# Gate tables with one operand in PSUM, whole-piece weight differences, and two batches' score transposes side by side

## The chip, the cores and the metric

The kernel runs on one core of a Trainium2 chip. The metric is device time in microseconds (us), taken as the median of several runs. With it comes one profiled execution, whose trace says when every instruction started and how long it took. The engines are TensorE (PE, with its weight loads as PEld), VectorE (DVE), ScalarE (ACT), GpSimd (POOL), and SyncE (SP), which starts most transfers. SBUF is the on-chip memory that all of them share, and PSUM the accumulator memory that TensorE writes.

## The reference

```python
def _attn_ref(x, w_r, w_i, b_r, b_i):        # x: 8 x 2496 x 256
    X = np.fft.rfft(x, axis=1)
    Yr = Xr @ w_r - Xi @ w_i + b_r
    Yi = Xr @ w_i + Xi @ w_r + b_i
    Yr = np.sign(Yr) * np.maximum(np.abs(Yr) - 0.01, 0.0)      # Yi alike
    return np.fft.irfft(Yr + 1j * Yi, n=2496, axis=1)

def _moe_ref(x, w_gate, w1, w2, capacity):   # x: 19968 x 256, 8 experts, capacity 80
    logits = x @ w_gate
    expert_idx = np.argmax(logits, axis=1)
    probs = np.exp(logits - logits.max(-1, keepdims=True))
    probs /= probs.sum(-1, keepdims=True) + 1e-09
    gate_w = probs[np.arange(N), expert_idx]
    out = np.zeros((N, D))
    for e in range(E):
        tok_idx = np.where(expert_idx == e)[0]
        # more than capacity: keep the 80 with the largest gate_w
        h = np.maximum(x[tok_idx] @ w1[e], 0.0)          # w1[e]: 256 x 1024
        out[tok_idx] = gate_w[tok_idx, None] * (h @ w2[e])
    return out
```

A Fourier transform along the sequence, a complex linear layer with a soft threshold, the way back, and then a mixture of eight experts in which each serves at most 80 of the 19968 tokens. All other rows of the output are zero.

## The kernel before, in words

**Main loop.** The sequence of 2496 is split as 39 x 64. The loop has 16 steps, two for each of the eight batches (`b` 0 to 7), and pipelines stages: a 39-point transform in f32, a 64-point transform, the complex weights with the soft threshold (L384 on TensorE; L392, L398, L401 on the others), and the way back, whose last part (`stageHB`, L534, L568, L572, with results in tiles `hs`) goes to the DRAM arrays `hd`. The step between, `stageD`, is L477, L480, L481 and L509 on TensorE with evictions L487 and L492 into `YO`.

**Gate tables.** The logits are linear in x, so the kernel carries eight gate columns through the inverse transform beside the data. For each batch `stageE1a` sums the gate columns to `G` and splits it into an f16 pair, `stageE1b` transforms them and sends them through DRAM (`gd`) to `gr`, and `stageE2` turns them into a table. A TensorE matmul leaves the logits L (78 partitions x 256, that is 32 tokens of 8 experts) in a PSUM tile. Then come the maximum `m` (L709), `d = L - m` (L710), `exp` on ScalarE (L711), its sum `q` (L712) and reciprocal (L713, L714), and the first place that holds the maximum, found with a table of ranks (L716, L717, L718). The last operation (L719) writes the gate of each token at its expert's place into the table, tile `gr`, or `Gs` for batch 6. `stageE3` transposes the table on TensorE (L725) and copies it from PSUM into `sall`, where all batches' tables lie side by side (L728 on VectorE for batches 6 and 7). Batch 7 goes by a path of its own, `stageG0`, `stageG1`, `stageE1c` and `back`, without the way through DRAM.

**Selection.** After the last table, VectorE selects tokens in `sall`: `level1` (L855 maxima, L856 their places, L864 products with a table `mod` into `V`, which TensorE L865 moves to the expert rows), index arithmetic on 128x16 tiles (L821 to L844), and rounds of maximum, replace and find (L882, L887, L888). `merge` and `choose` end it with L928, and TensorE turns its result into token positions (L933). Then GpSimd gathers rows by indirect transfers (L1020), TensorE runs the experts (L1105 and on), and the rows are scattered to the output (L1162).

**Weights.** Each expert's w1 and w2 come as f32 in four units of 128x1024. ScalarE makes the f16 part `wh` (L780; L777 and L774 for late ones), and the difference `wl = w - wh` in bf16 is GpSimd's (L788), for four units VectorE's (L783). Both parts lie in a tile `pair`.

**What sets the order.** The program is traced by a scheduler that keeps a modelled timeline. `tc.high_priority()` lets the instructions traced in it go ahead, and `tc.issue_after` holds instructions back until a named one has been placed. Each engine then executes its list strictly in order. PSUM tiles come from `psum()`, a ring of four buffers of 128x1024 f32; a buffer is free for its next user once the last instruction that reads or writes it is done.

Of the kernel before, what the change touches and what calls it, by code (L numbers as in the profile page):

```python
# [132 lines left out]
def fourier_mix_then_moe(ctx, tc, x, w_r, w_i, b_r, b_i, wg, w1, w2, t1, t2, vq, v3, v0, v1f, vt, sg, cst, cb, out):  # L133
    nc = tc.nc
# [4 lines left out]
    ek = ctx.enter_context(tc.tile_pool(name="ek", bufs=1))  # L139
# [18 lines left out]
    def psum():  # L158
        return ps[0].tile([128, 1024], F32, name="ps", bufs=ps[1])
# [17 lines left out]
    rank = const.tile([128, 8], F32, name="rank")  # L177
# [9 lines left out]
    unit = const.tile([128, 1], F32, name="unit")  # L187
# [170 lines left out]
    twos = []  # L358
# [223 lines left out]


    def stageE1a(b, Gs):
        G = ek.tile([128, 20, 8], F32, name="G", bufs=1)
        nc.vector.tensor_reduce(out=G, in_=Gs.rearrange("p c q (h e) -> p c e (q h)", e=8), op=ALU.add, axis=AX.X)
        gp = ek.tile([128, 2, 20, 8], F16, name="gp", bufs=2)
        nc.scalar.activation(gp[:, 0], G, AF.Copy)
        nc.vector.tensor_tensor(gp[:, 1], G, gp[:, 0], op=ALU.subtract)
        return gp  # L590

    v1h = const.tile([39, 78], F32, name="v1h")
    u7s = []
    uh7 = const.tile([128, 2, 5, 24], F16, name="uh7")

    def stageG0(b, YT):

        pt = psum()
        for j in range(11):
            c = j if j < 2 else 2 + (j + 4) % 9  # L600
            for eh in range(2):
                yt = lambda h: YT[:, eh, h, j].rearrange("p c k -> p (c k)")
                nc.tensor.matmul(pt[:, 16 * c:16 * c + 16], yt(0), wgi[:, eh, 128:144], start=(eh == 0), stop=False)
                nc.tensor.matmul(pt[:, 16 * c:16 * c + 8], yt(1), wgi[:, eh, 128:136], start=False, stop=(eh == 1))
        G = ek.tile([128, 20, 8], F32, name="gex")[:, :11]
        gp = ek.tile([128, 2, 20, 8], F16, name="gp", bufs=2)[:, :, :11]
        nc.vector.tensor_reduce(out=G, in_=pt[:, 0:176].rearrange("p (c h e) -> p c e h", h=2, e=8), op=ALU.add, axis=AX.X)
        nc.scalar.activation(gp[:, 0], G, AF.Copy)
        nc.vector.tensor_tensor(gp[:, 1], G, gp[:, 0], op=ALU.subtract)
        return gp  # L610

    def stageG1(b, R, eh):

        pt = psum()
        pv = pt[:, 0:120].rearrange("p (t k e) -> p t k e", t=5, k=3)
        for k in range(3):
            for x in range(3):
                nc.tensor.matmul(pv[:, :, k], R[:, 3 * x + k].rearrange("p c k -> p (c k)"), wgm[:, eh, x], start=(x == 0), stop=(x == 2))
        pv = pt[:, 0:120].rearrange("p (t f) -> p t f", t=5)
        if eh == 0:  # L620
            u7s.append(ek.tile([128, 20, 8], F32, name="G", bufs=1).rearrange("p a b -> p (a b)")[:, :120].rearrange("p (t f) -> p t f", t=5))
            nc.vector.tensor_copy(u7s[0], pv)
        else:
            u7 = u7s[0]
            nc.vector.tensor_tensor(u7, pv, u7, op=ALU.add)
            nc.scalar.activation(uh7[:, 0], u7, AF.Copy)
            ones.append(nc.vector.tensor_tensor(uh7[:, 1], u7, uh7[:, 0], op=ALU.subtract))

# [6 lines left out]
    def stageE1b(b, gp):  # L635
        pt = psum()

        for t, (tab, k) in enumerate(((vqs, 2), (vis, 8), (vqs, 14))):
            for v, h in ((0, 0), (0, 1), (1, 0)):
                nc.tensor.matmul(pt[:, 48 * t:48 * t + 48], tab[:, v], gp[:, h, k:k + 6, :], start=(v + h == 0), stop=(v == 1))  # L640
        special(pt[:64, 512:536], gp)
        gh = ek.tile([128, 21, 8], F32, name="gh", bufs=1)
        gu = ek.tile([128, 2, 48], F32, name="gdif")
        sc = 2.0 / S / XS
        g = float(np.sqrt(0.75))
        at = lambda a: gh[:, 6 * a:6 * a + 6].rearrange("p k e -> p (k e)")
        nc.scalar.activation(at(0), pt[:, 0:48], AF.Copy, scale=sc)
        nc.scalar.activation(gu, pt[:, 48:144].rearrange("p (t f) -> p t f", t=2), AF.Copy, scale=sc)
        nc.scalar.activation(gh[:64, 18:21], pt[:64, 512:536].rearrange("p (a e) -> p a e", a=3), AF.Copy, scale=sc)
        nc.vector.scalar_tensor_tensor(gu[:, 1], gu[:, 1], -1.5, at(0), op0=ALU.mult, op1=ALU.add)  # L650
        for a, f in ((1, g), (2, -g)):
            nc.vector.scalar_tensor_tensor(at(a), gu[:, 0], f, gu[:, 1], op0=ALU.mult, op1=ALU.add)
        nc.sync.dma_start(gd[b][0:21].rearrange("q n e -> n q e"), gh[0:64])
        nc.sync.dma_start(gd[b][21:39].rearrange("q n e -> n q e"), gh[64:128, 0:18])
        gr = ek.tile([78, 32, 8], F32, name="gr", bufs=1)
        for h in range(2):
            hops.append(nc.sync.dma_start(gr[39 * h:39 * h + 39], gd[b][:, 32 * h:32 * h + 32, :]))
        return gr
# [36 lines left out]
    def stageE2(b, gr, last=False):  # L695
        pt = psum()
        if last:
            for h in range(2):
                nc.tensor.matmul(pt[:78, :256], v1h if h else v1fs[:39], gr[:, :, 32 * h:32 * h + 32], start=(h == 0), stop=(h == 1))
        else:  # L700
            nc.tensor.matmul(pt[:78, :256], v1fs, gr.rearrange("p n e -> p (n e)"), start=True, stop=True)
        L = pt[:78, :256].rearrange("p (e n) -> p n e", e=8) if last else pt[:78, :256].rearrange("p (n e) -> p n e", e=8)
        bc = lambda t: t.unsqueeze(2).to_broadcast([78, 32, 8])
        m = ek.tile([78, 32], F32, name="gm")
        d = ek.tile([78, 32, 8], F32, name="gdif")
        ex = ek.tile([78, 32, 8], F32, name="gex")
        q = ek.tile([78, 32], F32, name="gq")
        sc = wkb.tile([128, 20, 2, 16], F32, name="Gs", bufs=2)[:78].rearrange("p a b c -> p (a b c)")[:, :256].rearrange("p (e n) -> p e n", e=8) if b == B - 2 else ek.tile([78, 8, 32], F32, name="gr", bufs=1)
        nc.vector.tensor_reduce(out=m, in_=L, op=ALU.max, axis=AX.X)  # L709
        nc.vector.tensor_tensor(d, L, bc(m), op=ALU.subtract)  # L710
        exps.append(nc.scalar.activation(ex, d, AF.Exp))  # L711
        nc.vector.tensor_reduce(out=q, in_=ex, op=ALU.add, axis=AX.X)  # L712
        nc.vector.scalar_tensor_tensor(q, q, 1e-9, unit[:78, 0:1].to_broadcast([78, 32]), op0=ALU.add, op1=ALU.mult)  # L713
        nc.vector.reciprocal(q, q)  # L714
        rk = rank[:78].unsqueeze(1).to_broadcast([78, 32, 8])
        nc.vector.scalar_tensor_tensor(d, d, 0.0, rk, op0=ALU.is_ge, op1=ALU.mult)  # L716
        nc.vector.tensor_reduce(out=m, in_=d, op=ALU.max, axis=AX.X)  # L717
        nc.vector.tensor_tensor(d, d, bc(m), op=ALU.is_equal)  # L718
        twos.append(nc.vector.tensor_tensor(sc.rearrange("p e n -> p n e"), d, bc(q), op=ALU.mult))  # L719
        return sc  # L720

    def stageE3(b, sc):
        pt = psum()
        for h in range(2):
            nc.tensor.transpose(pt[:, 128 * h:128 * h + 78], sc[:, 4 * h:4 * h + 4].rearrange("p e n -> p (e n)"), ident[:78, :78])  # L725
        o, i = sall[:, :, b], pt[:, :256].rearrange("p (h f) -> p h f", h=2)[:, :, :78]
        if b >= B - 2:
            nc.vector.tensor_copy(o, i)  # L728
        else:
            nc.scalar.activation(o, i, AF.Copy)  # L730
# [11 lines left out]
    def prepW(e, pool, name):  # L742
# [20 lines left out]
        def step(k, i):  # L763
# [4 lines left out]
            wh, wl = pairs[e][:, 0], pairs[e].bitcast(BF16)[:, 1]  # L768
            load(k, i)
            wt = got[k, i]  # L770
            c = 1024 * i
# [9 lines left out]
            if (e, k, i) in WV:  # L781
                with behind(("A", 'xv', (3, 4)[k])) if e == 7 and after else tc.issue_after(sels[-1].ins):
                    nc.vector.tensor_tensor(wl[:, k, c:c + 1024], wt, wh[:, k, c:c + 1024], op=ALU.subtract)  # L783
            else:

                m = 256 if e >= 2 else 1024
                for j in range(0, 1024, m):
                    nc.gpsimd.tensor_tensor(wl[:, k, c + j:c + j + m], wt[:, j:j + m], wh[:, k, c + j:c + j + m], op=ALU.subtract)  # L788
        return [(e, lambda k=k, i=i: step(k, i), lambda k=k, i=i: load(k, i)) for k in range(2) for i in range(2)]

    def weight(e, k):
# [699 lines left out]
    HBq.extend((pb, YO, pch, x) for x in (0, -1, 1, 2))  # L1491
    with tc.high_priority():
        sc = stageE2(b, gr, True)
    stageE3(p[0], sc6)
    doHB()
    YO1 = YO
    YO = wkb.tile([128, 2, 11, 256], F16, name="YO", bufs=2)
# [1 line left out]
        stageD(1, RR, YO, Gs, cls, False)  # L1499
    doHB(HBE)  # L1500
    with tc.high_priority():
        stageE3(b, sc)
    doHB(2)
    with tc.high_priority():
# [88 lines left out]
```

## Time and profile before

| | us |
|---|---|
| runs (median) | 637.53, 642.4, 640.14 (640.14) |
| the profiled execution | 635.39 |
| span of its instructions | 633.6 |
| outside the span | 1.8 |
| mean granted clock of TensorE | 0.931 of full |
| TensorE busy | 546.1 (86%) |
| VectorE busy | 406.7 (64%) |
| GpSimd busy | 315.2 (50%) |
| ScalarE busy | 302.7 (48%) |

Times in rows are from the start of the span. The main loop fills it to about 515; from there to 560 the tables of batches 6 and 7 and the selection run, and from 560 to the end gather, experts and scatter.

### The profile page before, as it was taken

Reading aid. Unit: us, or ns where it says so; the run is one execution under the profiler, and the core shown is the slowest. Engines: PE = TensorE matmul, PEld = TensorE weight load, DVE = VectorE, ACT = ScalarE, POOL = GpSimd, SP = SyncE. Lnnn points to the kernel's source line nnn. Section 1 sums busy time; section 2 is a strip of 40 time slices with the busy share of each in tenths; the row PEclk is TensorE's granted clock in tenths of the full one; section 3 lists DMA queues with packets and bytes.
Section 4 is the critical chain, followed back from the end, with each engine's and each line's share of the span. In section 5 each row is a group of like instructions: output and inputs, shape, how many; then the busy total and the mean of one; then the engine's idle time right before and its main releaser. Section 6 shows DMA issues by size and latency. Waiting matters only on the chain. (4 is left out here: it accounts for less than half of the span.)

```text
span 633.6 us, 12704 instructions
## 1 busy us (share of the span) xinstructions
PE 546.1 (86%) x4925; PEld 383.8 (61%) x4926; DVE 406.7 (64%) x748; ACT 302.7 (48%) x442; POOL 315.2 (50%) x310
## 2 busy tenths in 40 slices
PE   7366959999999999999999989987899984968791
PEld 2144527676766776686767657765677772526681
DVE  3432525466667667578656996875998847866860
ACT  2322525554545464554446544545566753601560
POOL 2000444444445453544445344575974697647681
PEclk8786978999999999999999999998999975969997
DMA  7796779689679968987997789699754584628830
GB/s 170 268 210 159 205 201 285 196 227 253 200 219 273 267 182 192 304 254 187 249 243 228 199 213 268 169 257 263 238 151 116 150 273 155 204 54 293 297 107 31
DMA packets 95912, 133.12 MB, mean 210 GB/s; under 512 B 26494, under 2 KB 77717, under 8 KB 93973
## 3 DMA queue, kind: packets, MB, share of 16 engines
q1 hardware_dynamic: 88341, 114.59, 67.2%
q10 hardware_dynamic: 5376, 8.39, 4.6%
q0 software_dynamic: 2128, 9.25, 4.3%
q8 instruction: 41, 0.67, 0.4%
q14 instruction: 26, 0.21, 0.1%
HBM read 69.57 MB, written 62.63 MB: 209 GB/s over the span
## 5 line engine op out<-in xcount | busy, mean ns | idle before, releaser
L384 PE MATMUL ps<-XT,WM 128*128 128x288 f16 (+1 forms) x1536 | 217.0, 298 | 8.0 <-DVE R L398 4.7
L384 PEld LDWEIGHTS <-WM 128*128 128x128 f16 x1536 | 149.2, 98 | 66.6 <-issue 12.8
L401 POOL TENSOR_TENSOR R<-R,sgs 128x576 f32<-128x576 f32 x28 | 35.8, 1280 | 183.5 <-DVE R L398 183.4
L398 DVE SCALAR_TENSOR_TENSOR R<-ps,thr,tp 128x674 f32<-128x674 f32 (+1 forms) x56 | 48.4, 864 | 96.1 <-ACT tp L392 94.0
L424 POOL TENSOR_TENSOR YT<-R,YT 128x1408 f16<-128x1408 f32 (+1 forms) x28 | 73.5, 2624 | 36.3 <-ACT YT L423 36.3
L392 ACT ACTIVATE tp<-ps,thr 128x674 f32<-128x674 f32 (+1 forms) x64 | 49.7, 777 | 87.5 <-PE ps L384 87.2
L282 PE MATMUL ps<-xt,t1f 117*117 117x512 f32 (+1 forms) x170 | 86.2, 634 | 3.9 <-DMA xt<-in_x 3.9
L328 PE MATMUL ps<-t2s,z 128*128 128x128 f16 (+1 forms) x320 | 60.3, 225 | 28.8 <-DMA z<-zd 21.1
L297 DVE TENSOR_TENSOR zs<-ps,zs 117x1024 f16<-117x1024 f32 (+1 forms) x45 | 51.0, 1135 | 27.2 <-ACT zs L296 26.1
L334 DVE TENSOR_TENSOR XT<-ps,XT 128x640 f16<-128x640 f32 (+2 forms) x64 | 51.9, 814 | 15.1 <-ACT XT L333 15.1
L296 ACT ACTIVATE zs<-ps 117x1024 f16<-117x1024 f32 (+1 forms) x45 | 43.0, 957 | 38.8 <-PE ps L282 34.7
L333 ACT ACTIVATE XT<-ps 128x640 f16<-128x640 f32 (+2 forms) x64 | 44.9, 702 | 33.9 <-PE ps L330 22.7
L329 PE MATMUL ps<-t2s,z 128*128 128x128 f16 (+1 forms) x320 | 60.2, 225 | 0.0
L330 PE MATMUL ps<-t2s,z 128*128 128x128 f16 (+1 forms) x320 | 60.1, 225 | 0.0
L328 PEld LDWEIGHTS <-z 128*128 128x128 f16 (+1 forms) x320 | 32.1, 100 | 37.5 <-DMA z<-zd 21.2
L423 ACT ACTIVATE YT<-R 128x1408 f16<-128x1408 f32 (+1 forms) x28 | 35.5, 1268 | 36.2 <-POOL R L420 35.9
L534 PE MATMUL ps<-YO,vqs 128*128 128x512 f16 (+1 forms) x252 | 49.5, 338 | 3.3 <-DVE R L398 3.3
L492 DVE TENSOR_TENSOR YO<-ps,YO 128x768 f16<-128x768 f32 (+1 forms) x50 | 45.3, 906 | 5.2 <-ACT YO L491 5.2
L282 PEld LDWEIGHTS ps<-xt,t1f 117*117 117x117 f32 (+1 forms) x170 | 29.2, 188 | 31.4 <-issue 30.3
L481 PE MATMUL ps<-wgi,YT 128*128 128x136 f16 (+1 forms) x302 | 42.8, 225 | 1.0 <-POOL YT L424 1.0
L534 PEld LDWEIGHTS <-vqs 128*128 128x128 f16 x252 | 24.9, 101 | 30.6 <-issue 14.4
L480 PE MATMUL ps<-wgi,YT 128*128 128x144 f16 (+1 forms) x302 | 43.2, 229 | 0.0
(274 smaller groups left out, 939.9 us busy)
## 6 DMA issues: line engine op xcount, KB each, us to landing
out<-zero SPq DMA_DIRECT2D x48, 384.0 KB
hd<-hs SPq DMA_DIRECT2D x94, 192.0 KB
zd<-zs SPq DMA_DIRECT2D x114, 156.0 KB
xt<-in_x SPq DMA_DIRECT2D x48, 312.0 KB
z<-zd SPq DMA_DIRECT2D x16, 576.0 KB
wt<-in_moe_w ACTq DMA_DIRECT2D x10, 512.0 KB
z<-zd SPq DMA_DIRECT2D x7, 704.0 KB
z<-zd SPq DMA_DIRECT2D x7, 640.0 KB
```

The source lines that it names most:

```text
L282: nc.tensor.matmul(pt[:K, 512 * j:512 * j + 512], t1f[:K, :K], xv[:, 2 * j:2 * j + 2], start=True, stop=True)
L297: nc.vector.tensor_tensor(zs[:K, :ng, 1, :], pv[:K, :ng], zs[:K, :ng, 0, :], op=ALU.subtract)
L328: nc.tensor.matmul(o, zz(0), t2s[:K, cl, 0, :], start=True, stop=False)
L329: nc.tensor.matmul(o, zz(0), t2s[:K, cl, 1, :], start=False, stop=False)
L330: nc.tensor.matmul(o, zz(1), t2s[:K, cl, 0, :], start=False, stop=True)
L334: nc.vector.tensor_tensor(ov(1), pv, ov(0), op=ALU.subtract)
L384: nc.tensor.matmul(pt[:, 512 * k:512 * k + n], WM[:, dh, m, wh, 128 * eh:128 * eh + 128], XT[:, dh, xh, c, c0 + n * k:c0 + n * k + n], sta ...
L392: nc.scalar.activation(fv(t), pv, AF.Relu, bias=thr[:, eh, ri, 0:1])
L398: nc.vector.scalar_tensor_tensor(fv(Rf), pv, thr[:, eh, ri, 1:2], fv(t), op0=ALU.add, op1=ALU.min)
L424: nc.gpsimd.tensor_tensor(yv(1), rv, yv(0), op=ALU.subtract)
L492: dvs.append(nc.vector.tensor_tensor(yol, yy, yoh, op=ALU.subtract))
L534: nc.tensor.matmul(o, tab[:, v], yo(h), start=(i == 0), stop=(i == 2))
```

## The change

There are five edits. Lines in the changed kernel are up to three higher or lower: `stageE2` there is L708 to L722, and `stageE3` is L728 and L731.

1. `stageE1a`, `stageG0`, `stageG1`: the sum `G` (or `u7`) goes to PSUM instead of SBUF. `stageE1a` takes a `psum()` buffer for it; the other two use free columns of a buffer that they hold.
2. `stageE1b`: ScalarE's scaled copy of 128x96 (L648) is gone, and VectorE's three operations read the PSUM tile.
3. `stageE2`: the chain for the first place starts from L again and works on PSUM tiles `best` and `place` beside L; the sum goes to PSUM as well. One operation is split in two, so that there are ten VectorE operations instead of nine. The three for the first place stand before the sum of the exponentials. The PSUM buffer is held to the last operation.
4. GpSimd's difference of a unit is one operation of 128x1024 for all experts; for experts 2 and up it was four of 128x256.
5. Batch 6's `stageE3` is written just ahead of batch 7's.

```diff
@@ stageE1a
-        G = ek.tile([128, 20, 8], F32, name="G", bufs=1)
+        G = psum()[:, :160].rearrange("p (c e) -> p c e", e=8)
@@ stageG0
-        G = ek.tile([128, 20, 8], F32, name="gex")[:, :11]
+        G = pt[:, 512:600].rearrange("p (c e) -> p c e", e=8)
@@ stageG1
-            u7 = u7s[0]
-            nc.vector.tensor_tensor(u7, pv, u7, op=ALU.add)
+            u7 = pt[:, 512:632].rearrange("p (t f) -> p t f", t=5)
+            nc.vector.tensor_tensor(u7, pv, u7s[0], op=ALU.add)
@@ stageE1b
-        nc.scalar.activation(gu, pt[:, 48:144].rearrange("p (t f) -> p t f", t=2), AF.Copy, scale=sc)
-        nc.vector.scalar_tensor_tensor(gu[:, 1], gu[:, 1], -1.5, at(0), op0=ALU.mult, op1=ALU.add)
+        nc.vector.scalar_tensor_tensor(gu, pt[:, 96:144], -1.5 * sc, at(0), op0=ALU.mult, op1=ALU.add)
         for a, f in ((1, g), (2, -g)):
-            nc.vector.scalar_tensor_tensor(at(a), gu[:, 0], f, gu[:, 1], op0=ALU.mult, op1=ALU.add)
+            nc.vector.scalar_tensor_tensor(at(a), pt[:, 48:96], f * sc, gu, op0=ALU.mult, op1=ALU.add)
@@ stageE2
-        nc.vector.tensor_reduce(out=q, in_=ex, op=ALU.add, axis=AX.X)
-        nc.vector.scalar_tensor_tensor(q, q, 1e-9, unit[:78, 0:1].to_broadcast([78, 32]), op0=ALU.add, op1=ALU.mult)
+
+        best, place, = (pt[:78, 256 * k:256 * k + 256].rearrange("p (n e) -> p n e", e=8) for k in (1, 2))
+        qs = pt[:78, 768:800]
+        rk = rank[:78].unsqueeze(1).to_broadcast([78, 32, 8])
+        nc.vector.tensor_tensor(best, L, bc(m), op=ALU.is_ge)
+        nc.vector.tensor_tensor(place, best, rk, op=ALU.mult)
+        nc.vector.tensor_reduce(out=m, in_=place, op=ALU.max, axis=AX.X)
+        nc.vector.tensor_tensor(best, place, bc(m), op=ALU.is_equal)
+        nc.vector.tensor_reduce(out=qs, in_=ex, op=ALU.add, axis=AX.X)
+        nc.vector.tensor_scalar(q, qs, 1e-9, None, op0=ALU.add)
         nc.vector.reciprocal(q, q)
-        rk = rank[:78].unsqueeze(1).to_broadcast([78, 32, 8])
-        nc.vector.scalar_tensor_tensor(d, d, 0.0, rk, op0=ALU.is_ge, op1=ALU.mult)
-        nc.vector.tensor_reduce(out=m, in_=d, op=ALU.max, axis=AX.X)
-        nc.vector.tensor_tensor(d, d, bc(m), op=ALU.is_equal)
-        twos.append(nc.vector.tensor_tensor(sc.rearrange("p e n -> p n e"), d, bc(q), op=ALU.mult))
+        twos.append(nc.vector.tensor_tensor(sc.rearrange("p e n -> p n e"), best, bc(q), op=ALU.mult))
@@ step
-                m = 256 if e >= 2 else 1024
-                for j in range(0, 1024, m):
-                    nc.gpsimd.tensor_tensor(wl[:, k, c + j:c + j + m], wt[:, j:j + m], wh[:, k, c + j:c + j + m], op=ALU.subtract)
+                nc.gpsimd.tensor_tensor(wl[:, k, c:c + 1024], wt, wh[:, k, c:c + 1024], op=ALU.subtract)
@@ the end of the main program
-    stageE3(p[0], sc6)
     doHB()
...
     with tc.high_priority():
+        stageE3(p[0], sc6)
         stageE3(b, sc)
```

**What moves.** On TensorE at the end of the main loop, before: `back` (L689), the logits of batches 6 and 7 (L699, tables `v1fs` and `v1h`), then at once the transposes of batch 6's table `Gs`.

```order
7502 L689 MATMUL ps<-ident,Gs 39x64 x8
7503 L699 MATMUL ps<-hs_6211,v1fs 78x256
7504 L699 MATMUL ps<-hs_6211,v1h 78x256
7505 L725 MATMUL ps<-ident,Gs 128x78 x2
7506 L568 MATMUL ps<-YO,v3s 128x512
7507 L568 MATMUL ps<-YO,v3s 128x256
7508 L477 MATMUL ps<-ident,R 128x128 x18
7509 L509 LDWEIGHTS v0s
...
7529 L509 LDWEIGHTS v0s
7530 L509 MATMUL ps<-YO,v0s 64x256
7531 L725 MATMUL ps<-ident,gr 128x78 x2
```

The same place now, on TensorE:

```order
7502 L688 MATMUL ps<-ident,Gs 39x64 x8
7503 L698 MATMUL ps<-hs_6186,v1fs 78x256
7504 L698 MATMUL ps<-hs_6186,v1h 78x256
7505 L568 MATMUL ps<-YO,v3s 128x512
7506 L568 MATMUL ps<-YO,v3s 128x256
7507 L477 MATMUL ps<-ident,R 128x128 x18
7508 L509 LDWEIGHTS v0s
...
7531 L509 MATMUL ps<-YO,v0s 64x256
7532 L728 MATMUL ps<-ident,Gs 128x78 x2
7533 L728 MATMUL ps<-ident,gr 128x78 x2
```

The transposes of batch 6 moved behind L568, L477 and all twelve L509, to stand directly ahead of batch 7's. Nothing stands between the logits and L568 any more.

On VectorE, the chains of batches 6 and 7 before, from the sum of batch 6's exponentials on:

```order
499 L712 TENSOR_REDUCE gq<-gex 78x32
500 L716 SCALAR_TENSOR_TENSOR gdif<-gdif,rank 78x256
501 L713 SCALAR_TENSOR_TENSOR gq<-gq,unit 78x32
502 L717 TENSOR_REDUCE gm<-gdif 78x32
503 L714 RECIPROCAL gq<-gq 78x32
504 L718 TENSOR_TENSOR gdif<-gdif,gm 78x256
505 L709 TENSOR_REDUCE gm<-ps 78x32
506 L719 TENSOR_TENSOR Gs<-gdif,gq 78x32x8
507 L710 TENSOR_TENSOR gdif<-ps,gm 78x256
508 L728 COPY sall<-ps 128x2x78
```

The two chains now, on VectorE (`ps<-` is an operation that writes PSUM; L690 is the copy of `back`):

```order
504 L715 TENSOR_TENSOR ps<-ps,gm 78x256
505 L690 COPY hs_6186<-ps 39x512
506 L716 TENSOR_TENSOR ps<-ps,rank 78x256
507 L717 TENSOR_REDUCE gm<-ps 78x32
508 L718 TENSOR_TENSOR ps<-ps,gm 78x256
509 L708 TENSOR_REDUCE gm<-ps 78x32
510 L709 TENSOR_TENSOR gdif<-ps,gm 78x256
511 L715 TENSOR_TENSOR ps<-ps,gm 78x256
512 L719 TENSOR_REDUCE ps<-gex 78x32
513 L716 TENSOR_TENSOR ps<-ps,rank 78x256
514 L720 TENSOR_SCALAR gq<-ps 78x32
```

The first-place operations of batch 6 stand ahead of its sum (row 512, L719), and the maximum and difference of batch 7 stand ahead of that sum too. Both copies into `sall` (L731) follow at rows 523 and 524, with the selection behind them.

On GpSimd, the last units ahead of the first gather, before and then now:

```order
187 L788 TENSOR_TENSOR pair_5779<-pair_6097,pair_5779 128x256 x8
188 L788 TENSOR_TENSOR pair_6550<-pair_6097,pair_6550 128x256 x12
189 L788 TENSOR_TENSOR pair_6575<-wt,pair_6575 128x256 x4
190 L788 TENSOR_TENSOR pair_6550<-pair_6097,pair_6550 128x256 x4
191 L1020 DMA tok<-cid,posA 128x4 x2
```

```order
186 L788 TENSOR_TENSOR pair_5779<-pair_6080,pair_5779 128x1024 x2
187 L788 TENSOR_TENSOR pair_6501<-wt,pair_6501 128x1024 x2
188 L788 TENSOR_TENSOR pair_6514<-pair_6080,pair_6514 128x1024 x4
189 L788 TENSOR_TENSOR pair_6527<-wt,pair_6527 128x1024
190 L1020 DMA tok<-cid,posA 128x4 x2
```

The same seventeen units stand between the main loop and the first gather, 68 pieces before and 17 now.

## Rows read from the trace of the kernel before

**Rows 1.** Windows, main loop: length; PE, PEld, DVE, ACT, POOL busy; clock; DMA share; GB/s

```profile
177.40:234.80 57.40, 57.23 (x500) 40.38 (x498) 38.64 (x57) 30.96 (x45) 27.77 (x25) 1.00 0.87 237
```

**Rows 2.** Timeline of PE, 520 to 545: start, duration, what ended its idle time

```profile
522.64 1.05 PE L699 MATMUL ps<-hs,v1h 39*78 39x256 f32 x2
532.85 0.52 PE L725 MATMUL ps<-ident,Gs 78*128 78x78 f32 x2 [9.16 <-DVE Gs L719]
533.17 2.85 PE L568 MATMUL ps<-YO,v3s 128*128 128x512 f32 x4
...
540.80 0.35 PE L725 MATMUL ps<-ident,gr 78*128 78x78 f32 x2
```

**Rows 3.** Windows, from batch 7's logits to the last transposes

```profile
522.50:539.00 16.50, 7.34 (x24) 5.08 (x23) 12.27 (x17) 6.34 (x10) 12.22 (x20) 0.50 0.51 157
```

**Rows 4.** Timeline of DVE, 523 to 537, the gate chains

```profile
524.42 6.38 DVE L716 SCALAR_TENSOR_TENSOR gdif<-gdif,rank 78x256 f32<-78x256 f32 x1
...
531.88 0.42 DVE L709 TENSOR_REDUCE gm<-ps 78x32 f32<-78x256 f32 x1
...
534.13 0.41 DVE L716 SCALAR_TENSOR_TENSOR gdif<-gdif,rank 78x256 f32<-78x256 f32 x1
...
535.77 0.97 DVE L719 TENSOR_TENSOR gr<-gdif,gq 78x256 f32<-78x256 f32 x1
```

**Rows 5.** Timeline of POOL, 503 to 549: weight differences

```profile
504.21 3.65 POOL L788 TENSOR_TENSOR pair<-pair,pair 128x256 bf16<-128x256 f32 x4 [4.07 <-ACT pair L780]
...
525.46 5.04 POOL L788 TENSOR_TENSOR pair<-pair,pair 128x256 bf16<-128x256 f32 x8
534.79 8.03 POOL L788 TENSOR_TENSOR pair<-pair,pair 128x256 bf16<-128x256 f32 x12 [4.28 <-ACT pair L777]
...
545.65 2.60 POOL L788 TENSOR_TENSOR pair<-pair,pair 128x256 bf16<-128x256 f32 x4
```

**Rows 6.** Timeline of DVE, 541 to 560, the selection

```profile
541.19 0.32 DVE L728 COPY sall<-ps 128x156 f32<-128x156 f32 x1 [4.45 <-PE ps L725]
...
542.79 0.93 DVE L864 TENSOR_TENSOR V<-mod,cv 128x256 f32<-128x256 f32 x1
...
545.76 0.59 DVE L827 SCALAR_TENSOR_TENSOR tk<-tk,tk 128x16 f32<-128x16 f32 x1
...
548.45 0.14 DVE L821 SCALAR_TENSOR_TENSOR tk<-tk,unit 128x16 f32<-128x16 f32 x1
...
559.10 0.81 DVE L928 TENSOR_TENSOR Gs<-pfb,eye 8x640 f16<-8x640 f32 x1
```

**Rows 7.** Waits of PE, 500 to 560: us in total, times, longest

```profile
PE ps L933 <- DVE Gs L928: 4.3, 1, 4.3
```

**Rows 8.** Groups by form, POOL: count, busy us, mean ns, idle before

```profile
L788 POOL TENSOR_TENSOR pair<-pair,pair 128x256 bf16<-128x256 f32 x48 | 34.1, 743 | 10.5 <-ACT pair L780 6.2 <-ACT pair L777 4.3
...
L788 POOL TENSOR_TENSOR pair<-wt,pair 128x1024 bf16<-128x1024 f32 x8 | 17.2, 2144 | 5.0 <-ACT pair L780 5.0
```

**Rows 9.** Groups by form, DVE, the same operation from PSUM and from SBUF

```profile
L710 DVE TENSOR_TENSOR gdif<-ps,gm 78x256 f32<-78x256 f32 x8 | 3.3, 414 | 0.2
...
L718 DVE TENSOR_TENSOR gdif<-gdif,gm 78x256 f32<-78x256 f32 x8 | 3.0, 381 | 0.0
```

**Rows 10.** Line L492: operation, count, duration ns min/median/max, first and last start, forms

```profile
L492 DVE TENSOR_TENSOR YO<-ps,YO x50: 680/948/959, 104.5 to 508.6; 128x768 f16<-128x768 f32 x42, 128x512 f16<-128x512 f32 x8
```

**Rows 11.** Line L719: the same columns

```profile
L719 DVE TENSOR_TENSOR gr<-gdif,gq x7: 600/2783/2805, 179.8 to 535.8; 78x256 f32<-78x256 f32 x7
```

**Rows 12.** Waits of PE, 230 to 420 (main loop)

```profile
PE ps L725 <- DVE hs L541: 1.4, 1, 1.4
PE ps L384 <- DVE hs L541: 1.4, 3, 0.5
```

**Rows 13.** Timeline of DVE, 502 to 508, ahead of batch 7's gates

```profile
502.44 0.76 DVE L409 TENSOR_TENSOR R<-R,sgs 128x576 f32<-128x576 f32 x1
...
506.29 1.04 DVE L409 TENSOR_TENSOR R<-R,sgs 128x576 f32<-128x576 f32 x1
```

More of the change, by code (lines that the diff above doesn't have):

```diff
@@ L642, in stageE1b @@
         gh = ek.tile([128, 21, 8], F32, name="gh", bufs=1)
-        gu = ek.tile([128, 2, 48], F32, name="gdif")
+        gu = ek.tile([128, 48], F32, name="gdif")
         sc = 2.0 / S / XS
```

## The prediction

> **What bounds the kernel now.** I read the busy shares by stretch first. In the main loop TensorE is the bound, 57.23 of 57.40 us in a typical stretch [rows 1], so VectorE work saved there is worth only what TensorE waits for. Behind the loop it is different, so I went to TensorE's timeline. The logits of batch 7 end at 522.64 + 1.05 = 523.69, and then TensorE sits idle for 9.16 us until it can transpose batch 6's table [rows 2]. All work behind that matmul waits with it, and runs afterwards at half clock: L568 at 533.17 to batch 7's transposes at 540.80, 7.63 us [rows 2]. The granted clock of that stretch is 0.50, the lower of its two levels [rows 3]. VectorE's timeline names the cause. L716 of batch 6 takes 6.38 us; the same operation for batch 7, with GpSimd between two runs, takes 0.41 [rows 4]. L716 reads two SBUF operands, and it begins and ends inside GpSimd's pieces: the last run of them ends at 525.46 + 5.04 = 530.50 [rows 5], and L716 ends at 524.42 + 6.38 = 530.80. Batch 7's chain, whose logits had been there since 523.69, starts at 531.88 behind it [rows 4].
>
> From there one chain of VectorE work sets the time: the last copy into `sall` at 541.19, the selection, its last operation L928 at 559.10 [rows 6], for which TensorE waits 4.3 us [rows 7], then the gather. I take the 73.6 us from there to the end of the span (633.6) as unchanged. So the question is by how much L928 comes earlier.
>
> **Step 1: the tables of batches 6 and 7 (edits 3 and 5).** Do the new chains escape the wait? In the trace of before, the 50 evictions L492 read one PSUM and one SBUF operand in a loop where GpSimd is busy half the time, and the longest takes 959 ns against a median of 948 [rows 10]. L719, with two SBUF operands, ranges from 600 to 2805 [rows 11]. Every operation of the new chain has at most one SBUF operand, so I take it as free of such waits. Its cost: batch 7's chain ran from 531.88 to the start of its last operation at 535.77 [rows 4], 3.9 us, with an operation and a copy of batch 6 among it (some 0.9) and 0.5 us for the last to add; I take 3.5 us for nine operations and 4 for ten. PSUM operands add 414 - 381 = 33 ns each [rows 9], 0.7 us over 20 operations. The two chains together take some 8.5 us and begin at about 522.5, so both tables are ready near 531. TensorE meanwhile does its 7.63 us from 523.69 on, still at half clock, and comes to the transposes at 531.3. Two transposes and two copies (0.52 and 0.35, 0.32 each) end near 533. Before, the second copy ended at 541.51: 8.5 us earlier.
>
> [...]
>
> What could take part of it back is the work ahead of batch 7's gates. L409 at 506.29 took 1.04 instead of the usual 0.76 us, because it met a GpSimd piece [rows 13]; with whole pieces it can meet 2.14 us instead of 0.74 [rows 8]. Bounds for what that and its neighbours delay: nothing and 3.4 us (two whole pieces less what they already wait); I take 1, the value nearest to the row. That leaves about 7.5 us at the second copy.
>
> **Step 2: GpSimd's whole pieces (edit 4).** A unit costs 4 x 0.743 = 2.97 us in pieces on average and 2.14 whole [rows 8]. In the tail, the ten units from 504.21 to 530.50 took 26.3 us and the five from 534.79 to 548.25 took 13.5 [rows 5]. Whole, the ten end at about 525.6. The five wait for ScalarE's copies, which before stood behind the exponential of batch 7, held back by L716; they will come a few us earlier, and with 5 x 2.14 = 10.7 us GpSimd ends at about 542.5 instead of 548.25. ScalarE's pace can put that anywhere between 540 and 545.
>
> **Step 3: the selection meets the pieces.** This is where most of step 1 goes. The selection's operations still have two SBUF operands. Before, while GpSimd worked, L864 took 0.93 and L827 0.59 us; when it had ended, the like of them took 0.14 (L821 at 548.45) [rows 6]. Each waited about one small piece. After, the first L864 is due near 534, and GpSimd works until 542.5. If each waits for one whole piece, L864, L864, L823 and L821 end at about 536, 538.3, 540.4 and 542.6, and L827 starts there instead of at 545.76: 3.1 us earlier. Behind it the rest runs free, which saves the waits of 0.4 us that two or three of them still had before. I take 3.5 us for L928. Lower bound: the first L864 is kept until GpSimd ends, as L716 was; then it ends at 542.9 instead of 543.72, and the operations behind save their waits of 0.3 to 0.5 us each, in all 2.5. Upper bound: it gets in wherever it asks, then all 7.5 us and some of today's waits arrive, about 9.
>
> [...] L716 was kept out for some 6 us, over nine pieces of 5.04 / 8 = 0.63 [rows 4, 5]. [...]
>
> **Step 4: the main loop (edits 1 to 3).** L719 loses about 2.2 us of waiting per batch on VectorE [rows 11], but with TensorE full that shows only where TensorE waits for VectorE behind it: 1.4 us once at L725, and 1.4 in three short waits [rows 12]. Bounds 0 and 2.8; I take 1.5. The ScalarE copy that `stageE1b` loses stands beside TensorE work: nothing. The PSUM buffers of `stageE1a`, `stageE1b` and `stageE2` are held longer, by one chain of about 4 us of VectorE work per batch. The ring has three other buffers meanwhile; I take nothing, and 2 us as a bound on the bad side.
>
> **Step 5: after 560.** Expert 7's differences on GpSimd get 3 x 0.8 = 2.4 us shorter. Nothing shown waits for them: nothing.
>
> **Sum.** 3.5 + 1.5 = 5.0 us. The profiled execution, 635.39 with its 1.8 us outside the span, would come to 630.4. It is 4.75 below the median of 640.14; against the median the forecast is 635.1. The runs spread by 4.9 us, so I treat 1% (6.4 us) as about what a measurement of this kernel can tell from no change.
>
> **Rivals.** *A, the selection gets in freely.* GpSimd's pieces become gaps when ScalarE cannot keep up, and an operation that waits gets in at once. For it: before, all operations of the selection got in at the next boundary [rows 6]. Against it: five whole pieces fall right into it. Then 9 + 1.5 us: 629.6.
>
> *B, all given back.* GpSimd's end stays at 548 because ScalarE's copies come no earlier, the selection waits for it, and main loop and weights are paced by transfers. For it: the idle time ahead of GpSimd's runs is all ScalarE's [rows 5, 8]. Against it: what held ScalarE back hung on L716. It gives 639 to 640.
>
> *C, slower: whole pieces starve VectorE ahead of batch 7's gates.* At 504 to 508 L407 and L409 have two SBUF operands, and ten units follow there without a gap [rows 5]. If L409 is kept out of the run, as L716 was, the gates of batch 7 and all of their work wait. It decides from a delay of 5 us on, more than two whole pieces; kept to the end of the ten units, 525.6 instead of 507.3, it costs 18.3 less the 5.0 gained: 653. Three or four pieces (6.4 to 8.6) give 641.5 to 643.7. Against it: the same operations got in at the first boundary before [rows 13].
>
> *D, the chains are not freed.* Operations with one PSUM operand would wait for GpSimd too, and for whole pieces. Each of the twenty could lose 2 us, TensorE would wait at its transposes until 540 or later, and the time would be 641 or so. L492 [rows 10] speaks against it.
>
> **How the numbers follow.** Forecast 0.42 (632 to 638), A 0.22 (626 to 632), B 0.20 (638 to 641.5), C 0.11, D 0.05. The range 627.5 to 642 leaves out C's greater part, some of D and the end of A, under 0.2. Faster by over 1% means below 633.7: nearly all of A and a third of the forecast, 0.35. Slower by over 1% means above 646.5: 0.08, the long end of C. The rest, 0.57, is within 1%.
>
> **What would show it.** L715 to L722 at 0.2 to 0.5 us each, whatever GpSimd does. TensorE without the 9 us gap, the transposes of 6 and 7 together at 531 to 533. GpSimd's pieces at 2.1 us, the last ending at 540 to 545. L864, L823, L821 at up to 2.2 us each, and L928 at 555 to 557 on the profiled execution's scale. The prediction is wrong if L928 moves by over 7 us or not at all, if L409 takes over 3 us, or if the stretch after L933 changes in length, since I left it as it is.

## The result and the profile after

| | before | after |
|---|---|---|
| runs, first comparison | 639.52 (637.53 to 642.4, 4 runs) | 632.54 (630.13 to 640.27, 4 runs) |
| ratio, 95% interval | | 0.9862 [0.9823, 0.9902] |
| again, with more runs (e1) | 643.9 (640.39 to 649.57, 35 runs) | 638.34 (635.42 to 644.05, 12 runs) |
| ratio, 95% interval | | 0.9907 [0.9876, 0.9938] |
| profiled execution, span | 635.39, 633.6 | 632.38, 630.5 |

Ratios leave out runs that lie over 1.5% above the fastest of their kernel: 640.27 here, three of twelve in e3 and two of twelve in e4. By the medians the change gains 7.0 us, by the larger comparison 643.9 x 0.0093 = 6.0, between 4 and 8. The forecast was 5.0. The profiled execution of the kernel before, 635.39, is faster than any of its 67 runs on record (the lowest is 636.0), while that of the changed kernel lies at its median; so the two profiles differ by less than the runs do.

TensorE after, in the place of [rows 2] (timeline: start, duration, what ended the idle time):

```profile
523.90 0.59 PE L698 MATMUL ps<-hs,v1h 39*78 39x256 f32 x2
524.42 1.56 PE L568 MATMUL ps<-YO,v3s 128*128 128x512 f32 x4
...
528.48 1.53 PE L477 MATMUL ps<-ident,R 128*128 128x128 f32 x12 [1.85 <-ACT hs L578]
529.85 1.59 PE L509 MATMUL ps<-YO,v0s 128*128 128x256 f16 x12
531.37 0.35 PE L728 MATMUL ps<-ident,Gs 78*128 78x78 f32 x2
531.56 0.30 PE L728 MATMUL ps<-ident,gr 78*128 78x78 f32 x2
...
557.75 0.28 PE L933 MATMUL ps<-ones8h,Gs 8*128 8x1 f16 x5 [5.39 <-DVE Gs L928]
```

The gap of 9.16 us is gone, and both batches' transposes stand at 531.4. L568 takes 1.56 us instead of 2.85, with a granted clock of 1.00 (524.40 to 531.90) instead of 0.50. The same window as in [rows 3] has 0.96, so 1.00 for nearly all of it:

```profile
522.50:539.00 16.50, 10.86 (x55) 6.31 (x54) 14.04 (x29) 15.28 (x22) 15.97 (x8) 0.96 0.86 273
```

VectorE after: the chains (compare [rows 4]), the second copy, and the selection (compare [rows 6]).

```profile
523.21 0.41 DVE L716 TENSOR_TENSOR ps<-ps,rank 78x256 f32<-78x256 f32 x1
...
530.53 0.61 DVE L722 TENSOR_TENSOR gr<-ps,gq 78x256 f32<-78x256 f32 x1
531.76 0.55 DVE L731 COPY sall<-ps 128x156 f32<-128x156 f32 x2 [0.62 <-PE ps L728]
...
533.59 2.31 DVE L864 TENSOR_TENSOR V<-mod,cv 128x256 f32<-128x256 f32 x1
...
536.29 1.88 DVE L864 TENSOR_TENSOR V<-mod,cv 128x256 f32<-128x256 f32 x1
538.09 2.09 DVE L823 CAST tk<-ci 128x16 f32<-128x16 uint32 x1
540.21 2.04 DVE L821 SCALAR_TENSOR_TENSOR tk<-tk,unit 128x16 f32<-128x16 f32 x1
542.29 2.04 DVE L827 SCALAR_TENSOR_TENSOR tk<-tk,tk 128x16 f32<-128x16 f32 x1
544.26 0.16 DVE L828 TENSOR_TENSOR tk<-tk,tk 128x16 f32<-128x16 f32 x1
...
556.88 0.81 DVE L928 TENSOR_TENSOR Gs<-pfb,eye 8x640 f16<-8x640 f32 x1
```

The second copy ends at 532.3 instead of 541.5, 9.2 us earlier. Then five operations take 1.9 to 2.3 us each, until GpSimd's last piece is done, and L928 is 2.2 us earlier. GpSimd (compare [rows 5]) shows the pieces that they meet; after its first four units it waits 5.0 us for a copy of ScalarE, and its last one ends at 544.3:

```profile
519.35 2.13 POOL L788 TENSOR_TENSOR pair<-pair,pair 128x1024 bf16<-128x1024 f32 x1 [4.99 <-ACT pair L783]
...
533.47 8.76 POOL L788 TENSOR_TENSOR pair<-pair,pair 128x1024 bf16<-128x1024 f32 x4
542.18 2.12 POOL L788 TENSOR_TENSOR pair<-wt,pair 128x1024 bf16<-128x1024 f32 x1
```

Ahead of batch 7's gates VectorE lost time (compare [rows 13]), and TensorE waited for it, 4.8 us in all where it had been 1.2 (second fence, its waits from 500 to 560):

```profile
506.17 1.53 DVE L407 TENSOR_TENSOR R<-tp,XT 128x576 f32<-128x576 f32 x1 [1.45 <-ACT XT L403]
...
507.81 2.48 DVE L409 TENSOR_TENSOR R<-R,sgs 128x576 f32<-128x576 f32 x1
```

```profile
PE ps L933 <- DVE Gs L928: 5.4, 1, 5.4
PE ps L618 <- DVE R L409: 4.8, 2, 2.5
```

To compare kernels I cut each trace at six TensorE matmuls and take the differences of their starts. They are the first, sixth and seventh logits that come by way of DRAM (L701 before, L700 after; batches 0, 5 and 6), batch 7's logits (L699 before, L698 after), the last transpose (L725 before, L728 after), and the matmul behind L928 (L933). Both tables of L699, `v1fs` and `v1h`, belong to batch 7; batch 6's logits are an L701, at 517.50 in the kernel before.

| us | 1st to 6th logits | 6th to 7th | to batch 7's | to last transpose | to L933 | to the end |
|---|---|---|---|---|---|---|
| before | 289.8 | 52.4 | 4.4 | 19.1 | 19.0 | 73.6 |
| after | 290.1 | 55.3 | 3.6 | 8.2 | 26.1 | 72.8 |
| e1 after again | 290.4 | 55.4 | 3.6 | 8.2 | 26.1 | 76.0 |
| e2 whole pieces only | 293.9 | 55.4 | 4.8 | 15.7 | 19.6 | 77.6 |
| e3 move only | 290.8 | 51.9 | 4.8 | 15.3 | 20.8 | 74.3 |
| e4 without whole pieces | 289.0 | 52.5 | 3.6 | 8.9 | 31.1 | 75.9 |
| e5 selection freed | 289.9 | 56.2 | 3.6 | 8.2 | 22.0 | 77.9 |
| e6 PSUM operands only | 293.4 | 52.8 | 3.6 | 12.3 | 27.7 | 79.6 |
| e7 e5, pieces of 256 | 288.0 | 52.9 | 3.6 | 8.3 | 21.9 | 78.0 |
| e8 pieces of 512 | 287.8 | 54.2 | 3.6 | 7.9 | 24.4 | 78.7 |
| e9 e7, own PSUM buffer | 292.4 | 52.3 | 3.6 | 8.9 | 18.6 | 75.7 |
| e10 256 for experts 2, 3 | 294.0 | 51.7 | 3.6 | 8.0 | 27.0 | 72.1 |

So the change takes 10.9 us out of the stretch of the chains, gives 7.1 back in the selection and 2.9 ahead of batch 7's gates. The four columns between the first and the last are steady; their sum is 94.9 us before and 93.2 after. The first column varies by 6.2 us over the profiles, with no order that follows the edits. The last varies by 7.5 us; by chip it is 74.3 to 77.6 on that of e1 to e4, 77.9 to 79.6 on that of e5 to e8, 75.7 and 72.1 on that of e9 and e10. On these three chips the kernel before runs at 643.9, 645.5 and 639.8. The changed kernel alone has 72.8 and, in e1, 76.0.

One thing behind L933 does follow the edits. In the three kernels that transpose batch 6's table in the old place (before, e2, e6) the first gather takes 4.0 to 4.1 us, in the nine others 1.85 to 1.96. It runs beside three VectorE operations of 128x1024 with two SBUF operands (L783 before, L786 after) and ends some 0.9 us after the third of them in those three kernels, but after the first of them in eight of the nine. GpSimd and VectorE behind L933, before and then after:

```profile
560.84 1.21 DVE L783 TENSOR_TENSOR pair<-wt,pair 128x1024 bf16<-128x1024 f32 x1
561.14 4.12 POOL L1020 DMA_INDIRECT tok<-cid,posA  x1 [12.89 <-DVE t2b L963]
561.98 2.34 DVE L783 TENSOR_TENSOR pair<-pair,pair 128x1024 bf16<-128x1024 f32 x2
...
565.57 0.97 POOL L1020 DMA_INDIRECT tok<-cid,posA  x1 [0.30 <-issue]
```

```profile
558.62 1.21 DVE L786 TENSOR_TENSOR pair<-wt,pair 128x1024 bf16<-128x1024 f32 x1
558.92 1.85 POOL L1020 DMA_INDIRECT tok<-cid,posA  x1 [14.62 <-DVE t2b L963]
559.75 2.34 DVE L786 TENSOR_TENSOR pair<-pair,pair 128x1024 bf16<-128x1024 f32 x2
...
561.08 1.87 POOL L1020 DMA_INDIRECT tok<-cid,posA  x1 [0.30 <-issue]
```

The second gather, measured from L933, ends at 6.6 to 7.2 us in the three and at 5.2 to 5.4 in the nine. Why the place of the transposes decides this, the traces do not show, and no run separates its share of the time.

### The profile page after: what moved, and what is told of

It reads as the page before. It is cut to its first block, busy times and chain, and to the rows that moved or that the text cites. A ratio compares the mean times of both kernels' runs of the same rounds, so it can differ in the third digit from the quotient of the medians.

```text
span 630.5 us, 12668 instructions
## 1 busy us (share of the span) xinstructions
PE 544.1 (86%) x4926; PEld 384.1 (61%) x4926; DVE 399.1 (63%) x756; ACT 301.5 (48%) x435; POOL 301.5 (48%) x250
## 5 line engine op out<-in xcount | busy, mean ns | idle before, releaser
L384 PEld LDWEIGHTS <-WM 128*128 128x128 f16 x1536 | 148.9, 98 | 64.6 <-issue 10.7
L492 DVE TENSOR_TENSOR YO<-ps,YO 128x768 f16<-128x768 f32 (+1 forms) x50 | 45.3, 906 | 7.8 <-ACT YO L491 7.8
```

The source lines that it names most:

```text
L384: nc.tensor.matmul(pt[:, 512 * k:512 * k + n], WM[:, dh, m, wh, 128 * eh:128 * eh + 128], XT[:, dh, xh, c, c0 + n * k:c0 + n * k + n], sta ...
L492: dvs.append(nc.vector.tensor_tensor(yol, yy, yoh, op=ALU.subtract))
```

## The experiments

Each ran beside the kernel before on the same chip, e1 to e4 on one, e5 to e8 on a second, e9 and e10 on a third. Ratios are to that, with 95% intervals; a percent is 6.4 us.

**e1, the changed kernel again.** 

> The changed kernel once more, to size its gain. Theory one (the gain is the freed chain of batches 6 and 7, minus what whole pieces cost the two-SBUF-operand operations): 4 to 9 us under the kernel before, transposes of both batches near 531.5, L928 near 557. Rival (the difference seen so far is mostly the spread of runs): 1 to 4 us under it.

0.9907 [0.9876, 0.9938], some 6 us, between 4.0 and 8.0. The rival's 1 to 4 us lie below that.

**e2, whole pieces alone (edit 4).**

```diff
-                m = 256 if e >= 2 else 1024
-                for j in range(0, 1024, m):
-                    nc.gpsimd.tensor_tensor(wl[:, k, c + j:c + j + m], wt[:, j:j + m], wh[:, k, c + j:c + j + m], op=ALU.subtract)
+                nc.gpsimd.tensor_tensor(wl[:, k, c:c + 1024], wt, wh[:, k, c:c + 1024], op=ALU.subtract)
```

> The kernel before with edit 4 alone (whole pieces on GpSimd). Theory one: L716 of batch 6 still waits for the end of a run of pieces, which comes up to 5 us earlier; L407 and L409 near 506 and the selection wait longer, as in the changed kernel (3 us and 1.4 us): in all between 3 us faster and 2 us slower. Rival (the gain comes from GpSimd being done sooner): 4 to 7 us faster, most of the whole change.

1.0022 [0.999, 1.0054]: nothing gained, so GpSimd's shorter work is not the gain by itself. My picture of L716 was wrong, though. It no longer waits for the end of a run but for one piece, and so does each operation behind it (VectorE of e2):

```profile
529.40 1.75 DVE L716 SCALAR_TENSOR_TENSOR gdif<-gdif,rank 78x256 f32<-78x256 f32 x1
531.08 2.10 DVE L713 SCALAR_TENSOR_TENSOR gq<-gq,unit 78x32 f32<-78x32 f32 x1
...
537.44 2.03 DVE L718 TENSOR_TENSOR gdif<-gdif,gm 78x256 f32<-78x256 f32 x1
539.50 2.43 DVE L719 TENSOR_TENSOR gr<-gdif,gq 78x256 f32<-78x256 f32 x1
```

**e3, the move alone (edit 5).**

```diff
-    stageE3(p[0], sc6)
     doHB()
...
+        stageE3(p[0], sc6)
         stageE3(b, sc)
```

> The kernel before with edit 5 alone (batch 6's transposes beside batch 7's). L716 still takes some 6 us and VectorE's chains end near 536.5, but TensorE does its 7.6 us of work meanwhile, so the transposes come near 537 instead of 540.8. Theory one: the copies into the table come 3 to 4 us earlier, and 2 to 4 us of that stay. Rival (the gain comes from GpSimd's work): no difference.

0.9923 [0.9882, 0.9965], 4.9 us of 643.9; by the medians of all its runs, 640.96 against 643.9, it is 2.9. L716 still takes 6.5 us here, but TensorE works meanwhile (VectorE, then TensorE, of e3):

```profile
525.49 6.47 DVE L716 SCALAR_TENSOR_TENSOR gdif<-gdif,rank 78x256 f32<-78x256 f32 x1
...
530.28 1.59 PE L509 MATMUL ps<-YO,v0s 128*128 128x256 f16 x12
534.12 0.33 PE L725 MATMUL ps<-ident,Gs 78*128 78x78 f32 x2 [2.24 <-DVE Gs L719]
538.04 0.49 PE L725 MATMUL ps<-ident,gr 78*128 78x78 f32 x2 [3.60 <-DVE gr L719]
```

This one line of the change reaches half or more of what the whole change does (5.6 us by the medians of e1), and by the ratios the two are not separated: the intervals of e1 and e3 overlap.

**e4, the changed kernel without whole pieces.** The diff of e2, backwards, on the changed kernel. 

> The changed kernel without edit 4 (four pieces of 256 for each unit again). Theory one: whole pieces cost more than they give. L407 and L409 near 506 wait less (about 3 us back), the selection's operations take 0.6 to 0.9 instead of 2 us each, GpSimd ends near 548: 0 to 4 us faster than the changed kernel, 6 to 11 us faster than the kernel before. Rival (GpSimd's earlier end is the gain): 3 to 6 us slower than the changed kernel.

0.9938 [0.9905, 0.997]: not faster than e1 as expected; it reads 2 us slower, which the intervals do not separate, and the trace does not show the rival's reason. The 6th to 7th logits came back as expected (52.5 us), the chains took 8.9. Then the first operation of the selection was kept out over 22 pieces in a row (VectorE, and GpSimd, of e4):

```profile
533.30 14.17 DVE L867 TENSOR_TENSOR V<-mod,cv 128x256 f32<-128x256 f32 x1
```

```profile
529.57 5.08 POOL L791 TENSOR_TENSOR pair<-wt,pair 128x256 bf16<-128x256 f32 x8
534.61 10.07 POOL L791 TENSOR_TENSOR pair<-pair,pair 128x256 bf16<-128x256 f32 x16
544.64 2.55 POOL L791 TENSOR_TENSOR pair<-wt,pair 128x256 bf16<-128x256 f32 x4
```

**e6, operands in PSUM alone (edits 1 to 3).** The diff of e4, and the two lines of e3 backwards. 

> Edits 1 to 3 alone (operands in PSUM; transposes of batch 6 where they were, pieces of 256). Theory one: the chain of batch 6 ends near 528.5 instead of 532.8, TensorE waits some 4 to 5 us for it instead of 9.2, then does its 7.6 us of work at half clock, so batch 7's transposes come near 537. With the selection's waits for small pieces that is 1 to 4 us under the kernel before. Rival (the order of TensorE is what counts): no difference, under 1 us.

1.0009 [0.9981, 1.0037]: no gain, as the rival said, but by another way. Batch 7's transposes came at 538.2, 6.8 us sooner after the logits than before (12.3 for 19.1), and the table was complete at 538.9. Then L864 (L867 here) met GpSimd's run and was kept out over 16 pieces, which took all of it back (VectorE, and GpSimd, of e6):

```profile
540.20 10.82 DVE L867 TENSOR_TENSOR V<-mod,cv 128x256 f32<-128x256 f32 x1
```

```profile
538.15 10.08 POOL L791 TENSOR_TENSOR pair<-pair,pair 128x256 bf16<-128x256 f32 x16
548.18 2.55 POOL L791 TENSOR_TENSOR pair<-wt,pair 128x256 bf16<-128x256 f32 x4
```

**e8, pieces of 512.** One profile. 

> The changed kernel with pieces of 512 for experts 2 and up. The question is how long a VectorE operation with two SBUF operands is kept out by back-to-back pieces. If it is a matter of one piece (the boundary rule), L864 near 533 takes at most 1.5 us. If runs of short pieces keep it out, as ten and more pieces of 256 did, it takes several pieces, 4 us or more.

One piece at a time, with 0.91 to 1.18 us for each of the first five operations that met one (VectorE of e8):

```profile
531.51 1.18 DVE L866 TENSOR_TENSOR V<-mod,cv 128x256 f32<-128x256 f32 x1
...
533.90 1.12 DVE L825 CAST tk<-ci 128x16 f32<-128x16 uint32 x1
535.06 1.08 DVE L823 SCALAR_TENSOR_TENSOR tk<-tk,unit 128x16 f32<-128x16 f32 x1
536.18 1.08 DVE L829 SCALAR_TENSOR_TENSOR tk<-tk,tk 128x16 f32<-128x16 f32 x1
```

**e5, the selection freed.** On the changed kernel:

```diff
@@ level1(1)
             pt = psum()
+            md = pt[:, 512:544]
+            nc.vector.tensor_copy(md, mod32)
+            nc.vector.tensor_copy(pt[:, 544:548], csts)
...
-                nc.vector.tensor_tensor(cm[:, h], mod32.unsqueeze(2).to_broadcast([128, 32, 8]), cv[:, h].unsqueeze(1).to_broadcast([128, 32, 8]), op=ALU.mult)
+                nc.vector.tensor_tensor(cm[:, h], md.unsqueeze(2).to_broadcast([128, 32, 8]), cv[:, h].unsqueeze(1).to_broadcast([128, 32, 8]), op=ALU.mult)
...
+        acc = lambda c: pt[:, c:c + 16].rearrange("p (h r) -> p h r", h=2)
+        new = (lambda dt: sb(dt)) if g == 0 else (lambda dt: (k.append(0), acc(560 + 16 * len(k)))[1] if len(k) in (1, 2, 4, 9) else sb(dt))
```

The last line puts four of the ten index tiles of `tokens` into columns of that buffer (`sb` makes an SBUF tile), so that no operation on them reads two SBUF operands. Not shown here: the index arithmetic gets three more tiles, so that it need not overwrite an operand, and it reads the constants from the copy in PSUM.

> The changed kernel, with the selection of level 1 freed as well: the table for L864, the constants, and every second of the index tiles lie in PSUM, so that no operation from the second copy into the table to the end of the indices reads two SBUF operands. Theory one (the selection gives back most of step 1 because its operations wait for GpSimd's pieces, some 10 us of waits in the changed kernel): L864 and the index operations take 0.15 to 0.45 us each, L928 comes 5 to 8 us earlier, and 3 to 8 us of it reach the end. Rival (behind the selection something else is late, the stores or the weights, or VectorE is not what sets the time): L928 earlier, but the end by less than 2 us.

0.9836 [0.9807, 0.9865], 4.6 us better than e1 by the ratios, with intervals that do not meet. No operation on the index tiles, and no product into V, takes over 0.5 us. The stretch to L933 is 22.0 instead of 26.1, 4.1 us shorter where 5 to 8 were expected; in it VectorE now waits twice for TensorE, 0.81 and 0.69 us.

**e7, the same with pieces of 256.** 

> The kernel of e5 with pieces of 256 again. Theory one: with the selection out of reach of GpSimd, whole pieces have only costs left on VectorE (L407 and L409 near 507, some 2 to 3 us), and small pieces cost GpSimd 7 to 10 us that nobody waits for; so 0 to 3 us faster than e5. Rival (GpSimd's own end or later weights set the time): 2 us or more slower than e5.

0.9829 [0.9799, 0.986]: level with e5. The 3 us ahead of batch 7's gates came back (52.9), but did not separate the two in the runs.

**e9, index tiles in a PSUM buffer of their own.** e5 and e7 put them in the buffer that TensorE writes V to, and in e7 VectorE waited there twice for TensorE, 0.78 and 0.69 us.

```diff
+            pk = psum()
-            md = pt[:, 512:544]
+            md = pk[:, 512:544]
...
```

The constants and the four index tiles move to `pk` as well.

> The kernel of e7 (pieces of 256, selection with a PSUM operand), with the index tiles in a PSUM buffer of their own instead of in the buffer that TensorE writes V to, so that the two no longer wait for each other. Theory one: the selection from the second copy to L933 falls from 21.9 to about 17 to 19 us; what reaches the end is less, since the stretch behind L933 was 4 us longer in e7 than before: 0 to 3 us faster than e7. Rival (a fourth of the PSUM ring is missed by TensorE's inverse transforms): same as e7 or up to 3 us slower.

0.9803 [0.9754, 0.9853], 627.67 us against 639.83, and 12.6 us under the kernel before by the ratio: the lowest ratio here, though its interval overlaps those of e5 and e7. The selection takes 18.6 us, as expected. L957 in it (L949 in the kernel before, where it takes 0.21 us) still has two SBUF operands and waits for the end of GpSimd's run at 551.4:

```profile
549.82 1.64 DVE L957 TENSOR_TENSOR Gs<-gh,t0b 8x64 f32<-8x64 f32 x1
```

**e10, pieces of 256 for experts 2 and 3 alone.** 

> The changed kernel with pieces of 256 for experts 2 and 3 alone, whole pieces for 4 and up. Theory one: L407 and L409 near 506 are served after a short piece, so the stretch from the sixth to the seventh logits falls from 55.3 back to about 52.5 us, while the selection still meets whole pieces at one wait each (about 26 us from the last transposes to L933): 1 to 4 us faster than the changed kernel. Rival (whole pieces cost nothing ahead of batch 7's gates, they only shift work): same as the changed kernel.

0.9888 [0.9841, 0.9936]. The stretch fell to 51.7 as expected, L409 to 1.03 us, and the selection stayed at 27.0. In the total, 1.2 us better than e1 by the ratios, this is not separated from it.

## Why the prediction was right, and where its terms were off

**What bounds the kernel, and step 1: right.** The chains ran at 0.2 to 0.6 us for each operation whatever GpSimd did; L722, which is L719's heir, took 599 to 611 ns in the seven main loop and tail places where L719 had taken up to 2805 [rows 11]. TensorE's gap was gone, and the second copy ended 9.2 us earlier, for 7.5 forecast and 8.5 in the working without its deduction (rows of L722 and, before and after, of L718):

```profile
L722 DVE TENSOR_TENSOR gr<-ps,gq x7: 599/608/611, 178.8 to 530.5; 78x256 f32<-78x256 f32 x7
...
L718 DVE TENSOR_TENSOR gdif<-gdif,gm x8: 349/357/562, 179.4 to 535.2; 78x256 f32<-78x256 f32 x8
...
L718 DVE TENSOR_TENSOR ps<-ps,gm x8: 402/428/429, 177.2 to 527.9; 78x256 f32<-78x256 f32 x8
```

Three sizes inside it were off. The deduction for L407 and L409 was taken as 1 and measured as 2.9 (6th to 7th logits, in all four profiles with whole pieces 55.3 to 56.2, with pieces of 256 51.7 to 52.9). Its upper bound of 3.4 was too low by its own words: two whole pieces less the 0.28 that L409 already waited are 4.0. And TensorE's 7.63 us were taken at half clock; the clock stayed at 1.00 from 524.40 to 531.90, and the same work took 6.95 us, with a wait of 1.85 for ScalarE in it. The gap alone is not shown to be what the clock answered to: before, it fell to 0.50 at 522.0, ahead of the gap, and stayed there to 539.1; in e4, e5 and e7, where the last transpose came 8.2 to 8.9 us after batch 7's logits, so without such a gap, it fell too, for a shorter while: its mean from 522.5 to 535 was 0.86 in each of them, and 1.00 in e1.

The third is the cost of a PSUM operand. The 33 ns come from means, and the 381 ns of L718 in [rows 9] hold one operation of 562 ns, which met a GpSimd piece. By the medians L718 costs 428 - 357 = 71 ns more with its operands in PSUM, and L710 420 - 357 = 63, so 1.3 us for twenty operations and not 0.7.

**Steps 2 and 3: right in mechanism, the term too large.** Each two-operand operation waited for one whole piece, and L827 started 3.5 us earlier than before, at 542.29, for 3.1 forecast. But GpSimd ended at 544.3 and not at 542.5 (540 to 545 were given), because it had stood still for 5.0 us ahead of 519.35 until ScalarE's copy came; so L827 too met a piece and took 2.04 us, and L928 gained 2.2 us instead of 3.5. Of the two readings that were weighed, one piece for each operation or a whole run as with L716, the first is what whole pieces and pieces of 512 showed: no operation waited for more than one piece, and the longest of the changed kernel beside them was 2.48 us (L409). My lower bound, taken from L716, did not occur with whole pieces. It did occur with pieces of 256, where one piece for each does not tell the time: four operations in these traces (before, e3, e4, e6) lost 9, 9, 22 and 16 pieces and got in only when the run ended.

**Edit 4 was priced with the wrong sign for its own stretch.** I counted whole pieces as a cost to the selection. Against small pieces that let every operation in at the next boundary (before, 0.93 us at most; e3, 0.64) they are. But with the tables ready at 531, small pieces kept the selection out (e4, 31.1 us instead of 26.1), and whole pieces were the safer choice there; the runs of e1 and e4 do not separate the two.

**Step 4: not seen.** The forecast had 1.5 us from the main loop. From the first to the sixth logits the kernels before and after took 289.8 and 290.1 us, and the others 287.8 to 294.0, so a term of 1.5 could not be read there if it existed. VectorE's 2.2 us per batch were saved; that TensorE, full there before [rows 1], passed none of it on is argued and not shown.

**Step 5: not nothing.** The stretch behind L933 was taken as unchanged, and a change in its length was named as a sign of being wrong. Its total, 73.6 before and 72.8 after, cannot decide that, since the changed kernel alone has 72.8 and 76.0. But inside it the first gather fell from 4.12 to 1.85 us, a term that the sum put at nothing.

**The sum: in part luck.** In the two profiled executions the steps give -10.9, +7.1, +2.9, -0.8, and -0.8 behind L933, -2.5 in all, with 0.6 more from the loop and the time ahead of it: 3.1 us of span. The runs show 6 or 7. In numbers the difference is that the profile of the kernel before lay 4.1 us under its median of 639.52, and that of the changed kernel 0.2 us under its own; which stretch was short in that one execution cannot be told. Of the forecast's two terms, 3.5 came out at 2.2 in these two profiles and 1.5 could not be seen. So the total of 5.0 came near the measured one without its terms adding up to it, and where the rest of the runs' gain comes from stays open; the gather is one candidate.

**The rivals.** A (the selection gets in freely) did not happen, but e5 and e9 brought most of it about by other means and show its price by the ratios: 4.6 and 6.7 us more. B's ground was half there: GpSimd did wait for ScalarE, 5.0 us, but it ended at 544.3 and not at 548. C's waits were real (L409 2.48 us) but one piece long. D was wrong: in the changed kernel's traces no operation with one PSUM operand took over 0.15 us longer than the shortest of its kind.

**What part of the change paid.** Step 1 put edits 3 and 5 into one term. The runs separate them: the move alone brings 4.9 us by the ratio (2.9 by all runs), the operands alone nothing, because they only carried the selection sooner into GpSimd's run. Step 1 took the freed chains for the gain; whether they pay once the selection is free as well, no run separates, since e5, e7 and e9 hold all edits to the chains and the move.

## What to carry to other kernels

When an engine waits in order for a slow chain (here TensorE, 9.16 us), first put other work ahead of the waiting instruction; one moved line brought half or more of what five edits did. When an edit frees a chain, look at what it brings forward: in e6 the freed chains carried L867 into GpSimd's run, where it took 10.82 us, so free the next users as well (e9: 12.6 us instead of 6, by the ratios). Read what a stalled operation was waiting for in the other engine's row, piece by piece, and count the pieces that passed: one for L827 of the changed kernel, 2.04 us, and 16 for L867 of e6.

## What the runs showed of the hardware

Some VectorE operations with two SBUF operands were kept out by back-to-back GpSimd operations far beyond one of them. With pieces of 128x256 (one each 0.63 us) four operations (before, e3, e4, e6) waited 6.0, 6.1, 13.8 and 10.4 us, each until GpSimd's run ended, while dozens of others in the same traces got in at the next boundary, after 0.1 to 0.5 us. With pieces of 128x512 (e8, at most 1.18 us from 531 to 538) and of 128x1024 (after, at most 2.48 us beside them) none waited for more than one.

The traces put the cases in an order. Count the time since the last such operation between GpSimd's pieces, or since the start of their run. All four came after 11 to 15 us, 18 to 24 pieces; L957 in e9 came after 10.7 us, 17 pieces, and waited 1.4 us, also to the end of the run. Of those that got in at the next boundary of such pieces, the longest had 6.1 us and 10 pieces ahead of it (L864 before, 0.93 us). With pieces of 512 (e8) and of 1024 (after), the first product into V got in after one piece, though GpSimd had run undisturbed for 10.3 and 10.6 us, 10 and 6 pieces. That orders what was seen; no run here varied it, so what decides stays open.

A cast with a single SBUF operand, L823, waited like the two-operand operations: 2.09 us against 0.16 when GpSimd was done (e4). The other way round, GpSimd's first gather beside three back-to-back VectorE operations with two SBUF operands took 4.0 to 4.1 us in the three kernels where it ended after the third of them, and 1.85 to 1.96 in the nine others, where it ended after the first in eight.
